# Attention kernel on one core: every third output store of four groups is sent as four stores over four DMA engines

## The chip, the cores and the metric

The kernel runs on one core of one Trainium2 chip. The core has a TensorE for matrix products (PE; its weight loads are shown apart as PEld), a VectorE (DVE), a ScalarE (ACT), a GpSimd (POOL) and a SyncE (SP), which here only issues transfers. Sixteen DMA engines move data between HBM and the on-chip memory SBUF. The metric is the time of one execution on the device in microseconds (us), lower is better. Before the change it is 348.19 us, the median of 3 runs that lie between 348.05 and 348.26.

## The reference

Grouped-query attention with a short query: 16 batches, 32 query heads, 8 key/value heads, 16 query rows, 2048 keys, head size 128, all in bf16.

```python
B, Hq, Hkv, Sq, Sk, D = 16, 32, 8, 16, 2048, 128
k = jnp.repeat(k, rep, axis=1)          # rep = Hq // Hkv = 4
v = jnp.repeat(v, rep, axis=1)
scores = jnp.einsum("bhqd,bhkd->bhqk", q, k) * D ** -0.5
p = _softmax(scores, axis=-1)
return jnp.einsum("bhqk,bhkd->bhqd", p, v)
```

The four query heads that share one key/value head have 4 x 16 = 64 query rows together. This is a *group*: 64 query rows against one K and one V of 2048 x 128. There are 128 groups. K and V are 64 MiB each; q and the output are 2 MiB each. So nearly all of the traffic is K and V, read once.

## The kernel before, in words

Two groups make a *pair* (64 pairs, `NP`), so that the 128 partitions hold 2 x 64 query rows. Two pairs, four groups, make a *step*: they share the key transposes, the score products, and one output tile.

For each pair:

- A K load of 1 MiB (128 partitions x 8 KB) and a V load of 1 MiB (packets of 4 KB) go into one of 15 buffers, `slot` (`NSLOT`). Both are issued on line 429.
- VectorE transposes K into `KT` in 32 x 32 blocks (line 354, two instructions for each group). TensorE makes the scores (line 452), ScalarE takes the exponential and its row sums (line 373), TensorE transposes the probabilities (line 462), VectorE or ScalarE copies them to SBUF (line 399), and TensorE multiplies them with V (line 468).
- VectorE or ScalarE multiplies the result with the inverse of the row sum and writes it to an output tile `O` (lines 388 and 390, the operation `nm` in the schedule). An output tile holds one step: 128 rows (two halves of 64 for the two groups of a pair) x 2 pairs x 128 columns. There are 9 such tiles (`NBO`), used in turn.

The query is loaded in 8 pieces of 256 KB and transposed ahead of its use (lines 360, 440, 399).

The order of the work on every engine is written out by a planner, `build_schedule` (line 135), which simulates the engines with a table of durations. The transfers are one list in a fixed order, made at the end of `make_ops` (lines 105 to 114), and SyncE issues them one after the other (`transfers`, line 402). It waits before each one until its buffer is free or its data ready; whatever stands behind it in the list waits too. V loads run 6 pairs behind the K loads (`LAG`), and the store of a step comes 12 further pairs later (`DSTORE`). For the most part a round of the list is K, V, K, V, store. Towards the end the K loads are over, and the list is two V loads and a store in turn. The last pair's V comes as two halves of 512 KB, and the stores 26 to 32 stand behind them.

The store of a step (`ST`, number `x`) is the part that is changed. For the steps 0 to 30 it is two transfers of 32 KB, one for each half of 64 partitions (line 426). In each transfer both sides have 64 rows as the slowest dimension, then the 2 pairs, then 128 contiguous elements, so that every contiguous piece is 256 B. The last two pairs are stored alone (line 421, and once from ScalarE, line 381).

A transfer adds 16 to its semaphore when it is complete. `point` (line 284) tells which semaphore and which value mean that an operation is done. The stores share 9 semaphores, one for each output tile; a paired store adds 32, a single one 16. The next normalization that writes the tile waits for that value, and so does the end of the kernel (`wait_stores`, line 314).

At the end the kernel counts whether all row sums lie in a safe range. If not, a second program, which subtracts the maximum, would run; with these inputs it doesn't.

## Time and profile before

| what | value |
|---|---|
| time, median of 3 | 348.19 us (348.05 to 348.26) |
| span of the profiled execution | 346.9 us |
| packets and bytes moved | 37349 packets, 139.21 MB, mean 401 GB/s |
| packets under 512 B | 11440 |
| HBM read, written | 136.31 MB, 2.10 MB |
| K load, issue to landing | 5.0 / 17.6 / 24.9 us (least, median, most) |
| V load, issue to landing | 12.1 / 17.4 / 25.8 us |
| paired store, issue to landing | 2.4 / 13.2 / 18.6 us |
| VectorE's waits for K loads | 92.8 us in all, 52 times, 3.7 us at most |

How to read it: the profile gives for each engine the time that it was busy and what ended its waits. It slices the span into 40 parts and shows the DMA engines' busy share in tenths, and the GB/s, of each. DMA traffic is listed by queue: q1 is the queue that SyncE issues on, q10 the one of ScalarE, and q8 and q14 carry instructions to the engines. "Issue to landing" is the time from the issuing instruction to the last of the semaphore's 16 increments; it includes the time that the transfer waits behind others. The 11440 packets under 512 B are 8192 packets of 256 B of the stores (8128 on q1, 64 on q10) and 3248 semaphore writes of 4 B (203 transfers x 16).

### The profile page before, as it was taken

The page shows a single profiled execution, that of the slowest core. Times are in us where ns is not written, and L with a number is a line of the kernel's source. Part 1 is how long each engine was busy: PE and PEld are TensorE (multiplying, and loading weights), DVE is VectorE, ACT ScalarE, POOL GpSimd, SP SyncE. Part 2 cuts the span into 40 slices and gives each one's busy share as a digit, 9 for nine tenths or more (in the row PEclk, how much of TensorE's full clock was granted, in tenths as well). Part 3 has the DMA queues.
Part 4 walks back from the last instruction along what each step waited for, and adds up shares of the span by engine and source line. Part 5 has one row for each costly group of instructions (what it writes and reads, how often), then busy time and mean ns, then how long its engine had stood idle before and what let it go on. Part 6 is the DMA issues. An engine that isn't in the chain of part 4 may idle for free.

```text
span 346.9 us, 11937 instructions
## 1 busy us (share of the span) xinstructions
PE 238.6 (69%) x5378; PEld 172.7 (50%) x5378; DVE 225.8 (65%) x377; ACT 226.6 (65%) x369; POOL 29.0 (8%) x35
## 2 busy tenths in 40 slices
PE   1568868756686668766687665865857757576785
PEld 1345646534464446543465453643645545454564
DVE  4867996874775666746666655767559476576544
ACT  4496887665586575946759646787558746477551
POOL 1310031000400004000040000400004000000000
PEclk9998999999899898999989989999899989899899
DMA  7999999999999999999999999999999999999983
GB/s 309 426 412 415 411 413 412 412 415 414 411 418 415 412 412 414 415 413 414 413 412 417 414 415 414 414 413 415 413 413 414 412 417 416 414 412 412 392 336 108
DMA packets 37349, 139.21 MB, mean 401 GB/s; under 512 B 11440, under 2 KB 11440, under 8 KB 29104
## 3 DMA queue, kind: packets, MB, share of 16 engines
q1 hardware_dynamic: 37216, 138.41, 98.9%
q8 instruction: 43, 0.70, 0.8%
q14 instruction: 10, 0.08, 0.1%
q10 hardware_dynamic: 80, 0.02, 0.0%
HBM read 136.31 MB, written 2.10 MB: 399 GB/s over the span
## 4 chain that ended last, share of the span: by engine, by line
DMA 72%; DVE 11%; PE 9%; ACT 6%; issue 1%; SPq 0%; ACTq 0%
DMA slot<-in_k_dram 72%; DVE KT L354 9%; PE O_ps L468 3%; ACT P L373 2%; PE PT_ps L462 2%; PE S_ps L452 2%; PE QT_ps L440 1%; ACT QT L399 1%; DVE PT L399 1%; ACT PT L399 1%; DMA Qn<-in_q_dram 1%; DVE O L390 1%; ACT L360 0%; ACT Qr L360 0%; DVE rowsum L379 0%
## 5 line engine op out<-in xcount | busy, mean ns | idle before, releaser
L354 DVE STREAM_TRANSPOSE KT<-slot 128x1024 int32<-128x1024 int32 x128 | 154.5, 1231 | 101.3 <-DMA slot<-in_k_dram 92.8
L373 ACT ACTIVATE P<-S_ps 128x1024 bf16<-128x1024 f32 x128 | 130.5, 1025 | 87.5 <-PE PT_ps L462 49.6
L462 PE MATMUL PT_ps<-ident,P 128*128 128x128 bf16 x1024 | 74.4, 229 | 83.1 <-DVE PT L399 44.0
L462 PEld LDWEIGHTS PT_ps<-ident,P 128*128 128x128 bf16 x1024 | 62.3, 102 | 104.7 <-DVE PT L399 53.7
L452 PE MATMUL S_ps<-KT,QT 32*64 32x512 bf16 x2048 | 75.9, 401 | 11.0 <-ACT P L373 9.7
L468 PE MATMUL O_ps<-slot,PT 128*64 128x128 bf16 x2048 | 76.7, 233 | 1.3 <-DVE O L390 1.0
L468 PEld LDWEIGHTS O_ps<-slot,PT 128*64 128x64 bf16 x2048 | 65.9, 119 | 17.8 <-issue 14.2
L399 ACT ACTIVATE PT<-PT_ps 128x1024 bf16<-128x1024 bf16 x60 | 61.1, 1019 | 3.0 <-PE PT_ps L462 2.1
L360 POOL COPY Qr<-Qn 128x1024 bf16<-128x1024 bf16 x28 | 28.0, 1042 | 235.2 <-DMA Qn<-in_q_dram 235.2
L399 DVE COPY PT<-PT_ps 128x1024 bf16<-128x1024 bf16 x68 | 45.2, 668 | 1.8 <-PE PT_ps L462 1.8
L452 PEld LDWEIGHTS S_ps<-KT,QT 32*64 32x64 bf16 x2048 | 28.1, 106 | 32.3 <-ACT P L373 12.9
L440 PE MATMUL QT_ps<-ident,Qr 128*128 128x128 bf16 x256 | 22.1, 236 | 10.2 <-ACT Qr L360 6.1
L399 ACT ACTIVATE QT<-QT_ps 128x1024 bf16<-128x1024 bf16 x23 | 23.5, 1023 | 7.3 <-PE QT_ps L440 7.3
L373 ACT ACTIVATION_READ_ACCUMULATOR P<-S_ps 128x1 f32 x128 | 25.9, 202 | 0.0
L440 PEld LDWEIGHTS QT_ps<-ident,Qr 128*128 128x128 bf16 x256 | 16.7, 105 | 16.5 <-issue 8.3
L388 ACT ACTIVATE O<-O_ps,rrec 128x128 bf16<-128x128 f32 x27 | 9.9, 367 | 11.6 <-PE O_ps L468 11.6
L390 DVE TENSOR_SCALAR O<-O_ps,rrec 128x128 bf16<-128x128 f32 x37 | 12.0, 324 | 5.5 <-PE O_ps L468 5.4
L399 DVE COPY QT<-QT_ps 128x1024 bf16<-128x1024 bf16 x9 | 10.9, 1209 | 1.8 <-PE QT_ps L440 1.8
L379 DVE TENSOR_TENSOR rowsum<-rhalf 128x1 f32<-128x1 f32 x64 | 8.5, 152 | 4.4 <-ACT P L373 4.4
L384 DVE RECIPROCAL rrec<-rowsum 128x1 f32<-128x1 f32 x64 | 8.5, 153 | 0.5
L360 ACT ACT_TABLE_LOAD x1 | 1.3, 1283 | 3.6 <-DMA Qn<-in_q_dram 3.6
L360 DVE COPY Qr<-Qn 128x1024 bf16<-128x1024 bf16 x2 | 1.3, 690 | 3.5 <-DMA Qn<-in_q_dram 3.5
(13 smaller groups left out, 4.2 us busy)
## 6 DMA issues: line engine op xcount, KB each, us to landing
slot<-in_k_dram SPq DMA_DIRECT2D x64, 1024.0 KB, 17.6
slot<-in_v_dram SPq DMA_DIRECT2D x63, 1024.0 KB, 17.7
Qn<-in_q_dram SPq DMA_DIRECT2D x8, 256.0 KB, 15.3
out_dram<-O SPq DMA_DIRECT2D x62, 32.0 KB, 13.2
slot<-in_v_dram SPq DMA_DIRECT2D x2, 512.0 KB, 12.3
out_dram<-O SPq DMA_DIRECT2D x3, 16.0 KB, 1.8
out_dram<-O ACTq DMA_DIRECT2D x1, 16.0 KB, 2.0
```

Of the source, the lines that this page charges most:

```text
L354: ins = eng.transpose(KT[p % NKT][:, gg, :, h], prog.slot(("K", 2 * p + gg))[:, J * 64 * h:J * 64 * (h + 1)])
L360: ins = eng.activation(dst, src, ACT.Copy) if me == "act" else eng.tensor_copy(dst, src)
L373: ins = eng.activation(P[p % 2][:, :].rearrange("m (r a h j) -> m h a r j", h=2, a=2, j=32)[:, h], src.rearrange("m (a r j) -> m a r j", a ...
L379: ins = eng.tensor_tensor(rowsum[:, p:p + 1], rhalf[:, p, 0:1], rhalf[:, p, 1:2], op=ALU.add)
L384: ins = eng.reciprocal(rrec[:, p:p + 1], rowsum[:, p:p + 1])
L388: ins = eng.activation(dst, src, ACT.Copy, scale=r)
L390: ins = eng.tensor_scalar(dst, src, r, None, op0=ALU.mult)
L399: ins = eng.activation(dst, src, ACT.Copy) if me == "act" else eng.tensor_copy(dst, src)
L440: ins = pe.transpose(QT_ps[:, 128 * i:128 * (i + 1)], Qr[:, x, i, :], ident[:, :],)
L452: ins = pe.matmul(S_ps[64 * gg:64 * (gg + 1), 512 * a:512 * (a + 1)], QT[c % 2][32 * a:32 * (a + 1), x, row:row + 64], kt[:, :, x // 2, p ...
L462: ins = pe.transpose(PT_ps[h][:, 128 * t:128 * (t + 1)], P[p % 2][:, 128 * r:128 * (r + 1)], ident[:, :])
L468: ins = pe.matmul(O_ps[64 * gg:64 * (gg + 1), 0:128], PT[p % NPT][:, r, 64 * gg:64 * (gg + 1)], prog.v_rows(p)[:, gg, r, :], start=(r == 0 ...
```

## The change

The stores 1, 4, 7, ... 28 (ten of the 31 paired ones) are issued in another form. Each of their two transfers of 64 partitions x 2 pairs becomes two, one for each pair (that is, one for each group), so four for the step. The destination of each is written with three dimensions: 4 heads x 16 rows x 128 elements, the slowest one of size 4, against 64 partitions on the source side. [...] The instruction is built by hand (`copy_on_four`), so that the three dimensions reach the hardware as they are written.

Bytes, contiguous pieces (256 B), the place of the stores in the list, and the waits before them stay. The value of the semaphore at which a store counts as complete is now summed over the stores that used it before: four parts of 16 for a changed store, two for another paired one, one for a single one.

```diff
+ON_FOUR = range(1, 31, 3)
...
-                full = 32 if op[0] == "ST" and op[1] < NP // 2 else 16
-                return self.sem_dma[op[0]][op[1] % n], 32 * (op[1] // n) + full if op[0] == "ST" else 16 * (op[1] // n + 1)
+                if op[0] != "ST":
+                    return self.sem_dma[op[0]][op[1] % n], 16 * (op[1] // n + 1)
+                parts = lambda x: 4 if x in ON_FOUR else 2 if x < NP // 2 else 1
+                return self.sem_dma["ST"][op[1] % n], 16 * sum(parts(x) for x in range(op[1] % n, op[1] + 1, n))
...
+    def copy_on_four(g, src, sem_, n):
+
+        sp = nc.sync
+        dst = bass.AP(of.tensor, of.offset + 64 * g * 128, [[16 * 128, 4], [128, 16], [1, 128]])
+        ins = mybir.InstDMACopy(
+            name=nc.get_next_instruction_name(), engine=sp.engine, queue="qSPDynamicHW",
+            ins=[sp.lower_ap_dma(src.rearrange("m (x d) -> m x d", x=1))[0]], outs=[sp.lower_ap_dma(dst)[0]], mode="Copy",
+        )
+        sp.add_instruction(ins).then_inc(sem_, n)
...
-                    sp.dma_start(of[64 * g:64 * (g + 2), :].rearrange("(p m) d -> m p d", p=2),
-                                 Osb[x % NBO][64 * gg:64 * (gg + 1), :, :]).then_inc(*prog_sem(prog, op))
+                    if x in ON_FOUR:
+                        for p in (2 * x, 2 * x + 1):
+                            copy_on_four(group_of(p, gg), o_tile(p)[64 * gg:64 * (gg + 1), :], *prog_sem(prog, op))
+                    else:
+                        sp.dma_start(of[64 * g:64 * (g + 2), :].rearrange("(p m) d -> m p d", p=2),
+                                     Osb[x % NBO][64 * gg:64 * (gg + 1), :, :]).then_inc(*prog_sem(prog, op))
```

## The prediction

> **What bounds the kernel now.** I began with the shares and slices of the page, then the queues, the chain, the groups, and last the end of the run in windows. The page's lines, engine by engine, then the DMA's slices and queues, the chain, the top group:

> ```profile
> PE 238.6 (69%) x5378; PEld 172.7 (50%) x5378; DVE 225.8 (65%) x377; ACT 226.6 (65%) x369; POOL 29.0 (8%) x35
> ...
> DMA  7999999999999999999999999999999999999983
> GB/s 309 426 412 415 411 413 412 412 415 414 411 418 415 412 412 414 415 413 414 413 412 417 414 415 414 414 413 415 413 413 414 412 417 416 414 412 412 392 336 108
> ...
> q1 hardware_dynamic: 37216, 138.41, 98.9%
> q8 instruction: 43, 0.70, 0.8%
> ...
> DMA 72%; DVE 11%; PE 9%; ACT 6%; issue 1%; SPq 0%; ACTq 0%
> ...
> L354 DVE STREAM_TRANSPOSE KT<-slot 128x1024 int32<-128x1024 int32 x128 | 154.5, 1231 | 101.3 <-DMA slot<-in_k_dram 92.8
> ```

> No compute engine is over 69% busy. The DMA engines are full from the second slice to the 37th, and 72% of the chain is K loads. So bytes over 16 engines set the pace, and what counts is the engine that finishes each load last. The instruction queue matters too: 43 packets, 0.70 MB, so 16 KB each; 0.8% of 16 x 346.9 us is 44 us, so 1.03 us a packet.

> The end of the run shows that the 16 engines are not equally loaded. Busy time by window (the last two columns are DMA share and GB/s), then the chain's tail (start, duration, what):

> ```profile
> 320.00:330.00 10.00, 6.73 (x130) 5.00 (x132) 5.49 (x10) 5.10 (x9) 0.00 (x0) 0.83 1.02 393
> 330.00:336.00 6.00, 5.27 (x144) 4.20 (x144) 2.94 (x6) 3.15 (x5) 0.00 (x0) 1.00 0.98 370
> 336.00:342.00 6.00, 5.03 (x124) 4.19 (x117) 3.16 (x9) 3.15 (x5) 0.00 (x0) 1.00 0.61 203
> ```

> ```profile
> 300.76 17.58 DMA slot<-in_k_dram
> ...
> 343.02 1.10 PE O_ps L468 x32
> 344.12 0.02 issue
> 344.15 0.35 DVE O L390
> ```

> The last V load was issued at 330.76, yet from 336 to 342 us only 0.61 of the engines' time is used: part of them is done and part is late. The semaphore updates in the trace resolve it, because each load is counted up by 16 increments, one as each engine finishes. In us:

> ```
> load, issued         1st      6th      7th      8th      9th      16th
> K     4.73         21.39    21.48    21.50    21.50    21.55    21.83
> K    52.57         72.30    72.75    73.33    73.60    73.90    74.33
> K   150.02        160.31   161.13   161.58   161.84   163.33   165.45
> K   300.76        310.16   311.14   311.96   312.93   316.20   318.34
> V   330.76        335.56   336.02   336.16   336.40   341.21   343.33
> ```

> The engines drift apart into **eight late ones**, two between, and **six early ones**, 7 to 8 us ahead by the end. The steps line up with the instruction packets: when one goes by (22.96, 31.3, 38.2 us and so on), one increment of the loads then in flight drops back about 1.55 us (at 24 us the last went from 0.33 to 1.85 us behind the middle), and after eight packets the same eight begin a second lap. 43 packets over 8 engines, 5.4 x 1.55 = 8.3 us, is the drift seen. The two between appear to take the 8 KB packets of the smaller instruction queue (seven before 300 us). The first eight never wait for work until about 330 us: the K load of 300.76 is picked up behind 9 us of queue even on the earliest. So the kernel runs at the pace of the late eight, while six engines carry slack of 318.34 - 311.14 = 7.2 to 8.2 us.

> [...]

> **The change part by part.** Ten of the 31 paired stores (1, 4, ... 28) change form. In the old form a paired store is two transfers; each engine gets 2 x 8 packets of 256 B and 2 semaphore writes. In the new form it is four transfers of 64 rows on four engines: those get 4 x 16 = 64 packets and 4 semaphore writes, the other twelve nothing.

> *Price of a store.* Two bounds. High: packet starts inside a store are 14.25 ns apart and a semaphore write takes 6 ns, so old 16 x 14.25 + 2 x 6 = 240 ns, new 64 x 14.25 + 4 x 6 = 936 ns. Low: by the landings, the step from a V load to the next K load is 2.49 us without a store between and 2.64 us with one (medians, 20 and 21 cases, the same at each of the 16 ranks), so a store really costs each engine 0.15 us, some of its packet time being absorbed; new, in proportion to the bytes, 0.60 us. I take 0.15 for what is removed, because it is measured on the late engines too, and keep 0.44 to 0.70 us as what each changed store adds to the four.

> *Removed from twelve engines:* 0.15 us a changed store. Before the K load of 300.76 there are 7 of them: 7 x 0.15 = 1.05 us (high 1.7). Before the last V load, 9: 1.35 us (high 2.1). If the late eight are among the twelve, all of this is on the path: each K load is waited for by DVE line 354 with DMA as releaser.

> *Added to four engines:* 7 x 0.44 to 0.70 = 3.1 to 4.9 us at that K load, 4.0 to 6.3 us at the last V. If the four are of the early six, they land at the latest at 311.14 + 4.9 = 316.0, below 318.34 - 1.05 = 317.3: hidden behind the late eight.

> *Two more issues per changed store* on SyncE, about 0.6 us each by the gaps between stores at the end. Queued behind them is the next K or V load, 1.2 us later. Even the early engines have 9 us of queue, the late ones 15, so the queue hides it. At the end store 25 stands ahead of the last two V halves: these are issued 1.2 us later, where early engines run short but late ones still have over 8 us queued. Store 28 falls where SyncE waits for results anyway.

> *Semaphore counts* change by what each ring entry adds; the output ring has 9 tiles of about 10 us each, so a store landing some us later delays no normalization. HBM bytes and compute are unchanged.

> *The end.* From the K load landing at 318.34 the chain is compute to 344.5 with no slack, and moves with that landing; the last multiplication also needs the last V half (343.33, inside the group that started at 343.02). The first comes 1.05 us earlier, the second 1.35. DVE still waits up to 2.1 us for each of the last K loads, so the compute can follow. Sum: about -1.2 us: 348.19 - 1.2 = **347.0 us**.

> **The rivals.**
> - *A: the first four are late engines.* For: eight of sixteen are late, and nothing here gives engine numbers. Against: [...] six early engines leave room for a run of four. Then each changed store adds 0.44 to 0.70 us to the bound: 7 to 9 of them, 3.1 to 6.3 us, to 351.3 to 354.5; middle 352.5.
> - *B: a between engine is among the four.* The later one (8th) lands at 312.93 + 3.1 to 4.9 = 316.0 to 317.8 against 317.3: gain 0.5 to 1.05, about 347.6.
> - *C: four engines carry small stores badly.* No trace shows 64 consecutive 256 B packets on an engine. At twice 14.25 ns a store is 1.8 us, 7 x 1.65 = 11.6 us against slack of 7.2 to 8.2: some 4 us later, 352. Against: groups of 16 run at even 14.25 ns steps with no sign of slowing.
> - *D: the tail doesn't follow.* The PE groups from 328 us on lie nearly end to end, so compute may take the gain back: 348.1. Against: its start is a wait for K.

> **How the numbers follow.** Forecast 0.60; A 0.17; B 0.09; C 0.06; D 0.08. Likeliest: 347.0. With the high price for what is removed (1.7 to 2.1 us) the forecast reaches 346.1, so the low end is 345.9. The high end must hold B, D and the mild part of A and C, where the four are less late than the worst: 350.0 leaves about 0.17 above. Faster by over 0.2% (0.7 us): the forecast, less a little for a gain under 0.7, and about half of B, 0.63; same: D, the rest of B, 0.14; slower: A and C, 0.23.

> **What would show it.** Right: the early increments of the K load near 300 us bunch closer to the late ones, four of them moved back by 3 to 5 us and the 16th about 1 us earlier; the DMA share from 336 to 342 us rises; 256 B packets per changed store stay 256 while semaphore packets fall by 16. Wrong by A or C: the 16th increment runs away from the 9th by several us and DVE's wait for K grows by as much. Wrong by D: K lands a microsecond earlier and the tail from there is longer than 26.2 us. What would make the forecast wrong is the one thing that I can't read: which engines are numbered first.

## The result, and the profile after

The changed kernel takes **351.12 us** (median of 4 runs, 350.92 to 351.57), beside 348.18 us for the kernel before in the same session (4 runs, 348.05 to 348.26). The ratio is 1.0086, with a 95% interval from 1.0069 to 1.0104: it is 2.9 us slower. Forecast was 347.0 us, in a range from 345.9 to 350.0.

The page after, with the lines that answer to those shown of before (engines, the DMA's slices and queues, the chain, the top group):

```profile
span 349.8 us, 11957 instructions
...
PE 237.7 (68%) x5378; PEld 171.2 (49%) x5378; DVE 226.4 (65%) x377; ACT 226.6 (65%) x369; POOL 29.0 (8%) x35
...
DMA  7999999999999999999999999999999999999991
GB/s 310 427 412 414 414 411 413 411 414 413 412 417 415 415 406 414 414 418 411 413 414 388 414 419 411 401 415 417 408 410 414 416 381 411 417 419 398 410 347 41
...
q1 hardware_dynamic: 37056, 138.41, 98.3%
q8 instruction: 43, 0.70, 0.8%
...
DMA 60%; PE 15%; DVE 11%; ACT 9%; SPq 2%; issue 1%; ACTq 0%
...
L357 DVE STREAM_TRANSPOSE KT<-slot 128x1024 int32<-128x1024 int32 x128 | 154.5, 1231 | 98.8 <-DMA slot<-in_k_dram 90.8
```

The compute engines did the same work. VectorE's wait for K loads *fell*, from 92.8 to 90.8 us. The DMA engines stay full for one slice longer: before, the last four slices moved 412, 392, 336 and 108 GB/s (the slices are now 8.7 us wide, 0.07 us wider), now 398, 410, 347 and 41. Queue q1 has 160 packets fewer, ten changed stores times 16 semaphore writes. The trace also shows over how many engines a part goes: each of the 40 parts left four increments of its semaphore that came with its data, and a single one for the other twelve, 0.38 to 0.47 us after the end of its issue (for store 1 the single ones at 85.74, 86.39, 87.84 and 91.27 us, the 16 with the data from 95.99 to 97.61), while every other transfer left 16. So four engines carry a part, as I meant it; that they are the first four by number, as the prediction calls them, no trace shows. Up to here everything is as forecast, and still the kernel is slower.

The loads come first. A load counts as landed with the last of its 16 semaphore increments. In us:

```
16th increment of            before    after   difference   forecast
K issued 300.76 / 298.86     318.34   317.42     -0.92       -1.05
the last K                   323.55   323.17     -0.38
the last V half              343.33   342.12     -1.21       -1.35

that first K load: 1st increment 310.16 before, 315.02 after
```

The 16 increments of that K load now lie between 315.02 and 317.42 us, where they lay between 310.16 and 318.34. The end of the loads moves as forecast. The early engines carry what the late ones shed, but that is not all that brings them together: of the six early ones only two are among the four (item 3 of the part on why the prediction was wrong), and yet no increment comes before 315.02, so the other four early ones, too, land at least 3.9 us later. Where SyncE is held up by the four parts of a store, the loads behind them go out late, and the early engines run out of work. After store 10 (8.6 us of issues) and store 19 (10.5 us), the first increment of the next load came 4.53 and 4.23 us behind that of the load before it, where 2.5 us is the usual step; the 16th took 2.50 and 2.98. Busy time in the stretches behind these two stores, before and then after (the last two columns are DMA share and GB/s):

```profile
188.00:192.00 4.00, 2.49 (x72) 1.90 (x64) 2.17 (x4) 2.84 (x5) 0.00 (x0) 1.00 1.03 416
284.00:286.00 2.00, 1.39 (x40) 0.57 (x36) 1.72 (x3) 1.62 (x3) 0.00 (x0) 0.97 0.99 410
```

```profile
188.00:192.00 4.00, 2.48 (x68) 1.98 (x64) 2.21 (x4) 2.83 (x6) 0.00 (x0) 1.00 0.93 357
284.00:286.00 2.00, 0.71 (x13) 0.72 (x14) 0.32 (x1) 2.00 (x4) 0.00 (x0) 1.00 0.88 345
```

Most of this idle time falls on engines that had a lead to lose, so the late ones, which set the pace, still gain. The same windows for the tail, after:

```profile
320.00:330.00 10.00, 6.40 (x162) 4.58 (x164) 5.01 (x12) 5.94 (x11) 0.00 (x0) 1.00 1.02 410
330.00:336.00 6.00, 5.60 (x151) 4.46 (x152) 2.80 (x8) 3.18 (x6) 0.00 (x0) 1.00 1.02 404
336.00:342.00 6.00, 4.57 (x109) 3.80 (x106) 3.38 (x13) 1.59 (x3) 0.00 (x0) 1.00 0.78 266
342.00:350.00 8.00, 0.76 (x18) 0.56 (x18) 0.40 (x2) 0.00 (x0) 0.00 (x0) 0.64 0.18 36
```

From 336 to 342 us the DMA share is 0.78, up from 0.61: the engines now finish more nearly together. From 342 us on there is little compute (0.76 us of PE, 0.40 us of DVE), while the span goes on to 349.8. What ends so late? The tail of the chain of waits, which follows the compute to its last instruction (start, duration, what), gives the first hint:

```profile
333.46 1.90 SPq L446
335.35 0.05 issue
335.40 6.72 DMA slot<-in_v_dram
342.12 0.04 issue
342.17 0.66 PE O_ps L485 x16
342.82 0.03 issue
342.85 0.35 DVE O L393
343.20 0.05 DVE flag L549
```

The compute ends at 343.25, 1.3 us *earlier* than before (344.55). And a new name stands in the tail of the chain: SPq, the sequencer of SyncE, which issued the last V half late. The timeline of SyncE at the end, before (start, duration with all gaps, line, what, count):

```profile
326.01 3.91 SPq L426 DMA_DIRECT2D out_dram<-O  x2
329.97 1.26 SPq L429 DMA_DIRECT2D slot<-in_v_dram  x2
331.33 10.97 SPq L426 DMA_DIRECT2D out_dram<-O  x10
342.99 2.00 SPq L421 DMA_DIRECT2D out_dram<-O  x3
```

and after, where line 413 is the new form:

```profile
325.55 7.42 SPq L413 DMA_DIRECT2D out_dram<-O  x4
333.02 2.85 SPq L446 DMA_DIRECT2D slot<-in_v_dram  x2
335.99 3.44 SPq L443 DMA_DIRECT2D out_dram<-O  x4
339.53 2.33 SPq L413 DMA_DIRECT2D out_dram<-O  x4
341.90 2.83 SPq L443 DMA_DIRECT2D out_dram<-O  x4
344.77 3.06 SPq L434 DMA_DIRECT2D out_dram<-O  x3
```

The first row is store 25, the second the two V halves, the rest the stores 26 to 32. Before, SyncE was done with the V halves at 331.23, and its last store went out at 344.53, when the compute gave it (344.55 is the end of the last VectorE instruction). After, it is done with the V halves at 335.87, then issues 15 store transfers nearly without a gap, and starts the last at **347.24, 4.0 us after the compute has ended**. The run ends 2.5 us after that issue; before, it ended 2.4 us after it. The 2.9 us are there: 2.71 in the last issue, the rest behind it. The last store itself is not slow: from the start of its issue to its last increment it took 1.72 us before and takes 1.84 now.

The sum of SyncE's tail can be made up from single issues. Store 25 and the V halves behind it end 4.64 us later (335.87 against 331.23). Store 28 has two transfers more, 0.6 us each: 1.2. Against this stand the waits for results that SyncE had before: 1.96, 0.69, 0.37 and 0.19 us between its last issues, 3.2 us in all. 4.64 + 1.2 - 3.2 = 2.6, and 2.71 was seen. That it fits so well is partly luck, since two further terms nearly cancel: the stores 26 and 27 were issued in 1.7 us less than before, and the stores 29 to 31 in 1.7 us more. Of the latter, 1.3 us lie in a single issue, the second transfer of store 31 (1.77 us, from 345.42), and while it lasted the instruction packets of the program's end went by (345.09 to 346.80).

Why did store 25 take 7.42 us? Its four issues last 2.75, 2.00, 0.55 and 1.63 us. That is not only this store. The timeline of SyncE round store 1, before and then after:

```profile
84.92 1.27 SPq L426 DMA_DIRECT2D out_dram<-O  x2
86.23 1.85 SPq L429 DMA_DIRECT2D slot<-in_k_dram  x1
```

```profile
84.70 6.15 SPq L413 DMA_DIRECT2D out_dram<-O  x4
90.89 2.43 SPq L446 DMA_DIRECT2D slot<-in_k_dram  x1
```

The parts' issues there last 0.66, 0.56, 1.40 and 3.40 us, so the later parts cost more than the first; the K load behind them goes out at 90.89 instead of 86.23.

**The issue theory.** Two things add up. Two issues more for each changed store are 1.2 us of SyncE. And parts on four engines fill the queues of these four: by an estimate from the packets and the increments, every part puts 64 / 4 = 16 packets of 256 B on each, where an old transfer put 128 / 16 = 8. An issue, so the theory, waits until these four have room, even when the other twelve have it; no trace shows how full a queue is. Early in the run the queue ahead would cover this on the late engines. At the end the long issues make the V halves and all stores behind them late, and the stores become the bound.

**The rival: the transfers.** The last stores are late because of what the DMA engines still carry, or because four engines carry 256 B packets badly; SyncE's long issues are only a symptom of that.

### The profile page after: what moved, and what is told of

Read it like the earlier page. It is cut to its first block, busy times and chain, and to the rows that moved or that the text cites. A ratio compares the mean times of both kernels' runs of the same rounds, so it can differ in the third digit from the quotient of the medians.

```text
span 349.8 us, 11957 instructions
## 1 busy us (share of the span) xinstructions
PE 237.7 (68%) x5378; PEld 171.2 (49%) x5378; DVE 226.4 (65%) x377; ACT 226.6 (65%) x369; POOL 29.0 (8%) x35
## 3 DMA queue, kind: packets, MB, share of 16 engines
q1 hardware_dynamic: 37056, 138.41, 98.3%
## 4 chain that ended last, share of the span: by engine, by line
DMA 60%; PE 15%; DVE 11%; ACT 9%; SPq 2%; issue 1%; ACTq 0%
DMA slot<-in_k_dram 58%; DVE KT L357 8%; PE S_ps L469 5%; PE PT_ps L479 5%; ACT P L376 4%; PE O_ps L485 3%; DMA slot<-in_v_dram 2%; ACT QT L402 2%; DVE PT L402 2%; ACT PT L402 2%; PE QT_ps L457 1%; SPq L443 1%; SPq L446 1%; DMA Qn<-in_q_dram 1%; DVE O L393 1%
## 5 line engine op out<-in xcount | busy, mean ns | idle before, releaser
L357 DVE STREAM_TRANSPOSE KT<-slot 128x1024 int32<-128x1024 int32 x128 | 154.5, 1231 | 98.8 <-DMA slot<-in_k_dram 90.8
L469 PE MATMUL S_ps<-KT,QT 32*64 32x512 bf16 x2048 | 76.8, 407 | 11.4 <-ACT P L376 10.1
L485 PE MATMUL O_ps<-slot,PT 128*64 128x128 bf16 x2048 | 75.1, 230 | 1.7 <-DMA slot<-in_v_dram 1.2
L485 PEld LDWEIGHTS O_ps<-slot,PT 128*64 128x64 bf16 x2048 | 64.2, 116 | 17.7 <-issue 12.8
```

The source lines that it names most:

```text
L357: ins = eng.transpose(KT[p % NKT][:, gg, :, h], prog.slot(("K", 2 * p + gg))[:, J * 64 * h:J * 64 * (h + 1)])
L469: ins = pe.matmul(S_ps[64 * gg:64 * (gg + 1), 512 * a:512 * (a + 1)], QT[c % 2][32 * a:32 * (a + 1), x, row:row + 64], kt[:, :, x // 2, p ...
L485: ins = pe.matmul(O_ps[64 * gg:64 * (gg + 1), 0:128], PT[p % NPT][:, r, 64 * gg:64 * (gg + 1)], prog.v_rows(p)[:, gg, r, :], start=(r == 0 ...
```

## The experiments

Eleven kernels. Ratios are to the kernel before in the same session, with the 95% interval. Lines are edits of the changed kernel unless said otherwise. "Last store" is the start of SyncE's last issue, "compute end" the end of the last VectorE instruction.

### The change without its last two stores

```diff
-ON_FOUR = range(1, 31, 3)
+ON_FOUR = range(1, 25, 3)
```

> Eight of the ten changed stores (1 to 22) keep the four-engine form, the last two (25 and 28) go back to the old form. Issue theory (the loss is SyncE at the end: the four-engine parts of the last two changed stores hold it up, the last stores stand behind them, while the loads themselves gain): about 347.0 us, 346.7 to 347.4, below both kernels, and the last K load lands about 1 us earlier than before. Bandwidth theory (each changed store costs DMA time, the twelve other engines run short while SyncE is held up): eight tenths of the loss stay, about 350.5 us.

Measured: 347.72 us (346.76 to 349.45, 22 runs; before 348.60, 75 runs), ratio **0.997 (0.9959 to 0.9982)**. That is 0.3 us above the range of the issue theory, in a session in which the kernel before, too, took 0.4 us more than in the first. SyncE's tail, in a run of 347.09 us:

```profile
325.45 3.97 SPq L443 DMA_DIRECT2D out_dram<-O  x2
329.81 1.98 SPq L446 DMA_DIRECT2D slot<-in_v_dram  x2
331.92 8.69 SPq L443 DMA_DIRECT2D out_dram<-O  x10
340.65 2.70 SPq L434 DMA_DIRECT2D out_dram<-O  x3
```

Store 25 takes 3.97 us, the V halves are out by 331.8, and the last store is issued at 342.88, with a compute end of 342.91. The eight changed stores that remain keep the gain of the loads (the K load near 300 us lands at 317.28), and nothing at the end eats it. This version is faster than both kernels.

### The last two alone

```diff
-ON_FOUR = range(1, 31, 3)
+ON_FOUR = range(25, 31, 3)
```

> Only the stores 25 and 28 are sent in the four-engine form, the other eight as before. Issue theory: the full loss at the end without the gain of the loads, 351 to 352.5 us. Bandwidth theory: two tenths of the loss, about 348.8 us.

Measured: 348.33 us (347.99 to 349.53, 22 runs), ratio 0.9992 (0.9982 to 1.0002): no change. The issue theory expected a loss, and neither expectation was met. SyncE's issues of store 25 and the V halves:

```profile
325.89 2.46 SPq L413 DMA_DIRECT2D out_dram<-O  x4
328.40 2.37 SPq L446 DMA_DIRECT2D slot<-in_v_dram  x2
```

The four parts of store 25 went out in 0.64, 0.61, 0.54 and 0.54 us, and the V halves at 328.40 and 330.28, no later than before. Here none of the eight stores before had added anything to the four engines, and the early ones were still 8 us ahead (the increments of the K load near 300 us run from 310.17 to 318.34). So a part on four engines is not slow to issue by itself. That it is held up when the four are already as full as the rest is the reading that fits. The theory is amended by that, and the two experiments together show that a loss needs both: earlier changed stores that use up the lead of the four, and a changed store close to the end.

### The parts on all sixteen engines

The same number of issues, in the ordinary form of a single group's store, which leaves 16 increments with its data (the last store before, from 346.05 to 346.25 us):

```diff
-copy_on_four(group_of(p, gg), o_tile(p)[64 * gg:64 * (gg + 1), :], *prog_sem(prog, op))
+sp.dma_start(*out_rows(p, gg)).then_inc(*prog_sem(prog, op))
```

> All ten changed stores are still sent as four transfers of 64 rows, but with 64 rows as the slowest dimension of both sides, so over sixteen engines. Issue theory in the form that a full queue of the four engines holds SyncE up: without four engines nothing fills, each part takes about 0.6 us to issue, 348.0 to 348.8 us. If the mere number of issues delays the end: 350.5 to 351.5 us. Bandwidth theory: no engine is left out or overloaded, 348.2 us.

Measured: 350.13 us (348.27 to 351.09, 22 runs), ratio 1.0028 (1.0012 to 1.0044), between the two expectations. (The times lie in two clusters, and the ratio, over all runs, is below that of the two medians, 1.0044.) The profiled run is one of the shorter (348.89). In it, the four issues of store 1 take 0.54, 0.60, 0.60 and 1.30 us (0.66, 0.56, 1.40 and 3.40 on four engines), and the K load behind them goes out at 87.91 instead of 90.89: the same number of issues, in the same place, without the hold-up. Store 25 takes 4.79 us instead of 7.42 (one issue of 2.68, three of about 0.6), the V halves go out at 330.65 and 331.28, and the K load near 300 us lands at 318.24, without gain. SyncE has no wait left after 337.19, and its last store starts at 344.55, with the compute end at 344.33: it only just keeps up. So the number of issues alone brings SyncE to the edge, and this version costs 0.28%; the form on four engines, which is all that differs, makes the rest. The two clusters lie near 348.8 (9 runs) and near 350.5 (13 runs). What decides between them wasn't found, and no trace is of the upper one, so that its loss, too, comes from the issues is not shown.

### The last four stores from ScalarE

SyncE's list is shortened: the stores 29 to 32 are issued by ScalarE after its own work.

```diff
+TO_ACT = (29, 30, 31, 32)
...
+            moved = [("ST", x) for x in TO_ACT]
+            self.progs["sp"] = [op for op in self.progs["sp"] if op not in moved]
+            self.progs["act"] = [op for op in self.progs["act"] if op[0] != "STA"] + moved + [("STA", 0)]
...
```

> All ten changed stores in the four-engine form as in the changed kernel, but the stores 29 to 32 are issued by ScalarE, idle by then, ahead of the one that it issues anyway. Issue theory: the last stores no longer stand behind SyncE's parts, 346.8 to 347.6 us. Bandwidth theory: about 351 us as in the changed kernel.

Measured: 349.95 us (348.56 to 350.45, 22 runs), ratio 1.0028 (1.0016 to 1.0039). Faster than the changed kernel, but most of the gain expected is missing. The timeline of ScalarE shows why:

```profile
338.34 3.86 ACTq L391 DMA_DIRECT2D out_dram<-O  x4
342.39 2.29 ACTq L396 DMA_DIRECT2D out_dram<-O  x3
344.71 0.62 ACTq L399 DMA_DIRECT2D out_dram<-O  x1
```

Eight issues on one engine take 7 us again, and the last starts 0.76 us behind the compute end (343.95), which is itself 0.7 us later than in the changed kernel. Its increments came in two sets, twelve between 346.40 and 346.56 and four between 347.71 and 348.12, while instruction packets ran from 345.67 to 346.98. The changed kernel has the same: of store 31, four of the 16 increments of the first transfer came up to 1.3 us after the others, and the issue of the second took 1.77 us instead of 0.6. The list was moved, not shortened.

### Each of the last two put back by itself

Store 28 in the old form, store 25 kept in the new; then the other way round:

```diff
-ON_FOUR = range(1, 31, 3)
+ON_FOUR = range(1, 28, 3)
```

> The stores 1 to 25 in the four-engine form, only 28 back in the old form. Theory of the late SyncE (store 25 is held up for 7 us by the full queues of the first four engines, the V halves and the last stores come 3 to 5 us late, the two extra issues of store 28 add 1.2 us, and late stores meet the instruction packets of the program's end): SyncE still has no time left, most of the loss stays, 349.3 to 350.8 us. If the extra issues of store 28 are the cause: back to about 347.3 us.

Measured: 350.40 us (349.98 to 351.51, 5 runs; before 348.40), ratio 1.0053 (1.004 to 1.0066). The V halves go out at 333.24 and 335.62, and SyncE's last store at 346.05 against a compute end of 343.64. As expected. SyncE's tail, in the longest of the five runs (351.51):

```profile
325.77 7.42 SPq L413 DMA_DIRECT2D out_dram<-O  x4
336.21 8.51 SPq L443 DMA_DIRECT2D out_dram<-O  x10
344.76 3.01 SPq L434 DMA_DIRECT2D out_dram<-O  x3
```

The last issue alone takes 1.72 us here, again with instruction packets going by (from 345.37), and the run ends 3.66 us behind its start.

```diff
-ON_FOUR = range(1, 31, 3)
+ON_FOUR = (*range(1, 25, 3), 28)
```

> The stores 1 to 22 and 28 in the four-engine form, only 25 back in the old form. Theory of the late SyncE: the V halves are issued near 330.3 us, SyncE reaches the last stores with some 1 us of slack less than without 28, 347.5 to 348.8 us. If store 28 is the cause: 350 us or more.

Measured: 349.48 us (349.26 to 350.4, 5 runs), ratio 1.0036 (1.0022 to 1.005), above what was expected. SyncE's last store is at 345.13, 0.36 us behind the compute end (344.77). But in this profile the loads had lost their gain: the K load near 300 us lands at 318.53. So only part of its loss is SyncE's, and why the loads shifted is open. Against the version with neither (0.997), store 25 costs 0.8% and store 28 at most 0.7%; store 28 is the less certain. Together they cost 1.2% (1.0086), less than the sum.

### Issues alone, no change to the engines

In the kernel before, the stores 26 to 30 are sent as four transfers over all sixteen engines, ten issues more at the end.

```diff
+ON_FOUR = range(26, 31)
...
+                    if x in ON_FOUR:
+                        for p in (2 * x, 2 * x + 1):
+                            sp.dma_start(*out_rows(p, gg)).then_inc(*prog_sem(prog, op))
```

> The kernel before, with the stores 26 to 30 alone sent as four transfers each over all sixteen engines: nothing is moved between engines and no load is touched, only ten issues of 0.65 us, 6.5 us of SyncE, are added behind the last load. Theory of the late SyncE: SyncE has about 3.5 us to spare there before, so the end comes some 3 us later, 350.5 to 352 us. Theory that the four engines' load is the cause: 348.2 to 348.6 us as before.

Measured: 355.98 us (355.8 to 356.45, 5 runs), ratio **1.0221 (1.0208 to 1.0235)**.

```profile
329.93 1.26 SPq L446 DMA_DIRECT2D slot<-in_v_dram  x2
331.29 17.09 SPq L441 DMA_DIRECT2D out_dram<-O  x20
348.43 1.87 SPq L434 DMA_DIRECT2D out_dram<-O  x3
```

The V halves leave as before, the compute ends at 344.54 as before, every transfer has the form that leaves 16 increments with its data (see the parts on all sixteen engines), and the run is 7.6 us longer. SyncE issues 23 transfers back to back and starts the last at 349.70, 5.2 us behind the compute. This shows without help of the change that the end can be bound by the issues, at 17.09 / 20 = 0.85 us each. The loss was more than expected because another 2 us pass between that issue and the end of the span, beyond the usual 2.4. They are not the stores': the last one landed at 351.55, 1.85 us after its issue as usual, and SyncE was through with its waits at 351.94, but its next instruction starts at 353.77. An instruction packet of 8 KB went by from 352.20 to 352.71, so SyncE most likely waited for its own instructions; that is not tested.

### Eight engines instead of four

```diff
-ON_FOUR = range(1, 31, 3)
+ON_FOUR = range(0, 24, 2)
...
-        dst = bass.AP(of.tensor, of.offset + 64 * g * 128, [[16 * 128, 4], [128, 16], [1, 128]])
+        dst = bass.AP(of.tensor, of.offset + 64 * g * 128, [[8 * 128, 8], [128, 8], [1, 128]])
```

> Every second store from 0 to 22 in four parts over the first eight engines (outer dimension 8, rows of 8), the rest in the old form; half as many packets for each engine and part as with four. If the first eight engines are the eight that aren't late: the late ones are relieved by 12 x 0.15 = 1.8 us, SyncE isn't held up at the end, 346.3 to 347.0 us, and the increments show two groups of eight that are 3.6 us closer. If some of the late engines are among the first eight: they carry 1.8 us more, 349.5 to 350.5 us.

Measured: 350.34 us (349.65 to 351.62, 6 runs), ratio 1.006 (1.0044 to 1.0076). With every second store up to 22 on eight engines, the K load near 300 us lands at 320.36, 2 us later than before, and its 15th and 16th increments stand 5.8 and 6.3 us behind the 8th. That two of the late engines are among the eight of this form, and run away as the prediction's rival A had it for four, is the reading that fits; no trace gives engine numbers. By the same reading the four of the changed kernel hold none of the late ones: there the 16th increment came 2.40 us behind the first.

### Relief for SyncE, with a control

If SyncE's list is the cause, taking the stores 26 to 30 off it must give the loss back, with store 25 still in the new form. GpSimd issues them (no work of its own after 320 us); they get semaphores of their own, and they leave SyncE's DMA queue (q1), where they stood behind the V halves.

```diff
-ON_FOUR = range(1, 31, 3)
+ON_FOUR = (*range(1, 26, 3),)
+TO_POOL = range(26, 31)
...
+            moved = [("ST", x) for x in TO_POOL]
+            self.progs["sp"] = [op for op in self.progs["sp"] if op not in moved]
+            self.progs["pool"] = self.progs["pool"] + moved
...
```

> The four-engine form for the stores 1 to 25 as in the changed kernel, but the stores 26 to 30 are issued by GpSimd, which is idle at the end, over sixteen engines and with semaphores of their own. The hold-up at store 25 and the late issue of the V halves stay. Theory of the late SyncE: SyncE has only the single stores left behind the V halves, the last ones go out as soon as they are computed, 346.9 to 347.8 us. If the four-engine stores cost the time in another way: 350 to 351 us as without store 28.

The control moves the same five stores with no store in the new form (`ON_FOUR = ()`):

> The control: no store in the four-engine form, the stores 26 to 30 from GpSimd as above. Before, SyncE had some 3.5 us to spare at the end, so taking ten issues off it gives nothing: 348.0 to 348.6 us. If the stores from GpSimd are a gain (or a loss) by themselves, it shows here.

and a third kernel has the eight early changed stores alone (`ON_FOUR = range(1, 25, 3)`) and the same move:

> The four-engine form for the stores 1 to 22, old form for 25, and 26 to 30 from GpSimd: the gain of the loads with SyncE free at the end. Theory of the late SyncE: about 1.1 us below the kernel before, 347.0 to 347.5 us, and steadier than with SyncE alone, where the last store went out with no time to spare.

| kernel | us (range, runs) | ratio to before (95%) |
|---|---|---|
| nine changed stores, five from GpSimd | 348.30 (347.82 to 348.72, 13) | 0.999 (0.9981 to 0.9998) |
| control, none changed, five from GpSimd | 349.00 (348.59 to 349.91, 18) | 1.0017 (1.001 to 1.0024) |
| eight changed stores, five from GpSimd | 347.81 (347.38 to 348.79, 18) | 0.9984 (0.9977 to 0.9991) |

The first has the same changed stores as the kernel above at 1.0053 (store 28 in the old form), and differs from it in who issues the five, with what comes with that (queue, semaphores, and the first two leave at 311 and 321 us). Its SyncE timeline:

```profile
326.67 7.43 SPq L431 DMA_DIRECT2D out_dram<-O  x4
334.15 2.93 SPq L464 DMA_DIRECT2D slot<-in_v_dram  x2
342.79 2.20 SPq L452 DMA_DIRECT2D out_dram<-O  x3
```

Store 25 holds SyncE for 7.43 us as it did, and the V halves are as late (334.15), but behind them SyncE waits for the compute again, and its last store starts at 344.52 with the compute end at 344.55. The loss of 0.53% is gone. If the bytes that the DMA engines carry were the cause, another issuer would give no relief, since the bytes and their engines are the same. Another queue alone would not help either: the changed kernel's last store took 1.84 us to land, 0.12 more than before, so nothing to speak of was queued ahead of it, and the stores that ScalarE issued, above, went by another queue too (q10), without relief: the kernel took 349.95 us. GpSimd's stores themselves cost 0.6 us (the control, which was expected at no change), so against the control the gain is 0.27% with nine changed stores and **0.33%, 1.2 us, with eight**: what the loads had promised. Both versions lie above the ranges expected for them (346.9 to 347.8 and 347.0 to 347.5), by about what the control costs.

## Why the prediction was wrong

1. *DMA engines set the pace, eight of them late: right.* The drift and its cure are seen in the increments: spread 8.18 us before, 2.40 after, at the same K load. Part of the closing up is idle time of the early engines, which I had not foreseen.
2. *0.15 us removed from twelve engines for each changed store: right.* Seven stores gave 0.92 us (0.13 each; 1.05 forecast), nine gave 1.21 (1.35 forecast). The low price, measured on landings, was the better one.
3. *What is added to four engines is hidden: right for landings, but barely.* Four parts of a store landed some 0.19 us apart on an engine (the first store's at 95.99, 96.17, 96.35 and 96.56 us), so a changed store takes about 0.77 us of each of the four, inside the forecast's bounds of 0.60 and 0.94. The parts of the first store landed on two engines with the early increments and on two with the 7th and 8th (the first part 0.17 to 0.21 us behind 95.82, 95.83, 96.57 and 96.82 us, all increments of the V load just ahead), so the four hold the two engines that I called between and two early ones. This is rival B's arrangement. At the K load near 300 us the gain was near the forecast's all the same, as the eighth had room (before, it came 5.4 us ahead of the 16th). At the last K load it was only 0.38 us: there the 16th increment came 0.8 us behind the 15th, and 2.52 us, one load's step, behind the last part of store 22 (320.65), so one of the four had most likely become the last.
4. *"Two more issues per changed store ... the queue hides it": **the step that failed***, on two counts. I priced an issue at 0.6 us, about the least that one of a paired store took, and let store 25 make the V halves 1.2 us late. Its issues took 7.42 us instead of 3.91, and SyncE was done with the V halves 4.64 us later. And I took the queue for a reserve of transfers that hides a late issue, when a queue that is full is, by the reading above, also what makes the issue late. The trace of before had this: line 426's issues took 595 ns at least, 966 in the median and 6641 at most. I named only the gap between stores at the end. Nor was the reserve so large: the 9 us that I gave the early engines ran from issue to landing, with the load's own 2.5 us in them, and the four issues of a changed store took up to 10.5 us (store 19), so early engines ran out of work.
5. *"Store 28 falls where SyncE waits for results anyway": wrong as a consequence.* Those waits, 3.2 us in all, were used up by store 25 before store 28 was reached. I costed the two edits one by one, and each against the same slack.
6. *The end: -1.2 us: right for the compute, wrong for the run.* The compute ended 1.3 us earlier. I let the span's end follow it, but 13 store issues stand behind the V halves on SyncE (15 after the change), and the last of them ends the run. It went out late by 2.71 us, 1.3 of them in an issue held up among the instruction packets that I had only priced for the loads. Before, it came out with the compute (344.53 and 344.55), so it looked like part of the same chain.
7. *The rivals.* A, C and D did not happen: no increment ran away (at the K load near 300 us the 16th came 0.96 us behind the 9th), the four parts of a store landed at an even pace (some 0.19 us each), and the compute followed (1.3 us earlier). None of them was SyncE, although the issues were in the list of parts. A rival that took a step "at nothing" and asked "what if not?" could have found it: two changed stores at the end add four issues, 2.4 to 3.9 us at 0.6 to 0.97 us each, against slack of 3.2 us.

**Not settled.** Which limit of the queue holds the issue up: that it is the four engines' own room fits the second and third experiment (fast when the four are ahead, fast on sixteen), but no run measured the limit. Also open are the two clusters of the third, the shift of the loads with store 25 put back, and how much of the loss the instruction packets at the end make by themselves.

## What to carry to other kernels

Count the issues of the engine that sends transfers as a stage of its own, above all behind the last load: so many issues by the time that they take *in this trace's median*, against the waits that this engine has there, all edits together. A store spread over four engines was held up here when, by the reading above, these were no longer ahead (7.42 us for the four issues of store 25, 2.46 in the kernel with the last two alone), and it held up everything behind it in the list; so put such transfers where many loads are still ahead, and leave the last ones in the wide form (0.9970 instead of 1.0086 here). And when the compute ends earlier but the span later, look at what was issued last.
